# A segment-sum kernel: one source bucket per row of parts 0 and 1 fetched by an indirect row transfer instead of a one-hot product

## The chip, the cores and the metric

The kernel runs on one core of one Trainium2 chip. The metric is the device time of one execution in microseconds. Before the change, three runs took 1863.13, 1871.68 and 1876.03 us, median 1871.68.

## The reference

A graph layer: neighbour features are summed at each destination node, scaled by the inverse degree, and added to the node's own term.

```python
nsum = _segment_sum(x[src], dst, N)
h_neigh = nsum * deg_inv[:, None]
return x @ w_self + h_neigh @ w_neigh
```

There are N = 12500 nodes, 64 features and 800000 edges with random `src` and `dst`. So 800000 rows of x have to be gathered and added up.

## The kernel before, in words

The gather and the sum are both done by TensorE as products with one-hot matrices. For that the edges are sorted first. Each edge becomes a key; keys are grouped into **buckets**: a bucket is a block of 164 destination nodes (there are 77) crossed with a block of 128 source nodes (there are 98), 7546 buckets in all. Each bucket has 128 slots, which hold most of its edges (106 on average); what doesn't fit goes to the "leftovers".

The first 800 us sort: VectorE (DVE) sorts each partition's 6250 keys, then runs are gathered, merged, gathered again and merged, until each of 128 rows holds a fixed number of consecutive buckets. The work is split in three **parts** with 29, 20 and 10 buckets per row (`KPRS`), so part 0 is buckets 0 to 3711, part 1 from 3712 to 6271, part 2 the rest. Only part 0 is ready when the loop over buckets starts. The merges of parts 1 and 2 (L316, L328) are issued on DVE inside that loop, a slice per tile, with a budget per tile that `PACE` gives (an estimate in ns) less what other work of the tile has spent (`self.spent`).

When a part's rows are merged, `find_and_gather` counts bucket limits and fetches a window per bucket (L742), and `decode_buckets` turns the windows into two things: the source numbers within a block (0 to 127), stored to a DRAM table `sl` with one row of 128 per bucket (L794; on SP's queue for part 0, on POOL's for the other parts), and the destination numbers, transposed on TensorE into the SBUF table `dlT`.

The bucket loop is `nodes`. It goes over tiles of 8 buckets (950 tiles):

- `one_hots` (L924) prepares chunks of 28 buckets. Four DMAs on SP's queue (L933) copy the chunk's rows of `sl` to all 128 partitions (`slb`, 3 buffers). DVE compares with the partition's number and gets the source one-hots `ohs` (L935), and compares the columns of `dlT` with a row of numbers for the destination one-hots `ohd` (L940).
- `gather` multiplies each bucket's `ohs` with the 128 node rows of its source block (L966), which yields the bucket's 128 gathered rows in PSUM (`ct`, 8 buckets wide, 3 buffers). ScalarE (ACT) copies them to SBUF as f16 (`xg`, L976); in part 2 DVE takes some of these copies (L974). A row has 128 f16: 64 high parts and 64 low parts of the features.
- `sums` comes a few tiles later and multiplies `xg` with `ohd`, in two halves of 64 partitions, adding up in PSUM `acc` over the 98 buckets of a destination block (L1047). Six blocks (588 buckets, an "octet") share one accumulator; then it is copied out (L1054), multiplied with the weights (L1114), scaled (L1117) and added to the output by an accumulating DMA from POOL's queue (L1123).
- Leftover edges come in groups of 128: `pick` fetches their x rows from the DRAM copy `xt` by an indirect DMA that POOL issues (L997, tile `lx`, 5 buffers), `spread` makes their one-hots (L1006), `add` adds the product (L1015).

The order on each engine is the order in which the Python code issues the instructions. POOL (GpSimd) has one queue for all its work: the leftover gathers, the row gathers of a merge (L565, eight per part, one per tile, each followed by a small memset), the window gathers (L742), the stores to `sl` of parts 1 and 2 (L794) and the outputs (L1123). An instruction that waits holds up all behind it. A leftover gather into a buffer that is still in use waits for the product that reads it (L1015).

## Time and profile before

| | us |
|---|---|
| median of three runs | 1871.68 |
| the profiled execution's own time | 1856.37 |
| its span | 1854.6 |
| bucket loop, parts 0 and 1 | about 805 to 1665 |
| bucket loop, part 2 | about 1665 to 1837 |

| engine | busy us | share of the span |
|---|---|---|
| TensorE products (PE) | 986.6 | 53% |
| VectorE (DVE) | 1718.2 | 93% |
| ScalarE (ACT) | 1116.7 | 60% |
| GpSimd (POOL) | 576.2 | 31% |

How to read the lines below: a line of a group names line, engine, operation, tiles written and read, shapes and count; then the busy time in us and the mean duration in ns; then the idle time of the engine just before these instructions, and what ended it. `ct<-xh,ohs` means that `ct` is written from `xh` and `ohs`. PEld is TensorE's weight load. A table by stretches gives, for each stretch, the busy time and count of each engine, the granted TensorE clock, the share of the DMA engines and GB/s. A wait line reads: who waited, for whom, us in total, times, longest. The chain of waits is followed back from the last instruction; "issue" is time in which the engine waited for nothing that the profile shows.

### The profile page before, as it was taken

The page shows a single profiled execution, that of the slowest core. Times are in us where ns is not written, and L with a number is a line of the kernel's source. Part 1 is how long each engine was busy: PE and PEld are TensorE (multiplying, and loading weights), DVE is VectorE, ACT ScalarE, POOL GpSimd, SP SyncE. Part 2 cuts the span into 40 slices and gives each one's busy share as a digit, 9 for nine tenths or more (in the row PEclk, how much of TensorE's full clock was granted, in tenths as well). Part 3 has the DMA queues.
Part 4 walks back from the last instruction along what each step waited for, and adds up shares of the span by engine and source line. Part 5 has one row for each costly group of instructions (what it writes and reads, how often), then busy time and mean ns, then how long its engine had stood idle before and what let it go on. Part 6 is the DMA issues. An engine that isn't in the chain of part 4 may idle for free.

```text
span 1854.6 us, 54153 instructions
## 1 busy us (share of the span) xinstructions
PE 986.6 (53%) x23413; PEld 851.9 (46%) x23413; DVE 1718.2 (93%) x1718; ACT 1116.7 (60%) x1587; POOL 576.2 (31%) x447
## 2 busy tenths in 40 slices
PE   3046000000000000058979979897898899888996
PEld 1015000000000000057868868776887788777885
DVE  6999999999999999989989999998898799978885
ACT  5263000113001005458979989899999899977885
POOL 2000000055502005404456535473332523532331
PEclk7567555555555555579989999999999999999998
DMA  5207100021002002169978888996889788977894
GB/s 174 54 0 169 39 0 0 38 79 51 18 4 73 10 0 82 47 216 266 274 249 253 251 248 254 296 282 227 264 250 284 234 265 242 326 200 257 274 268 118
DMA packets 176789, 307.79 MB, mean 166 GB/s; under 512 B 127885, under 2 KB 133596, under 8 KB 175772
## 3 DMA queue, kind: packets, MB, share of 16 engines
q1 hardware_dynamic: 98268, 275.58, 44.9%
q0 software_dynamic: 78272, 28.65, 9.6%
q8 instruction: 185, 3.03, 0.7%
q14 instruction: 64, 0.52, 0.1%
HBM read 277.01 MB, written 26.52 MB: 164 GB/s over the span
## 4 chain that ended last, share of the span: by engine, by line
DVE 19%; PE 13%; DMA 11%; issue 10%; SPq 5%; POOL 4%; ACT 4%; DVEq 0%; POOLq 0%; ACTq 0%
DMA slb<-sl 10%; PE ct L966 7%; DVE u L328 7%; PE acc L1047 5%; SPq L933 5%; DVE ohs L935 4%; DVE ohd L940 3%; ACT xg L976 2%; DVE u L362 2%; POOL u L565 1%; POOL lx L997 1%; POOL out L1123 1%; DVE u L316 1%; DMA sl<-l 1%; PE acc L1015 1%
## 5 line engine op out<-in xcount | busy, mean ns | idle before, releaser
L976 ACT ACTIVATE xg<-ct 128x1024 f16<-128x1024 f32 x919 | 862.6, 1074 | 104.4 <-PE ct L966 80.0
L966 PE MATMUL ct<-xh,ohs 128*128 128x128 f16 x7546 | 532.6, 224 | 87.9 <-DVE ohs L935 23.7
L966 PEld LDWEIGHTS <-ohs 128*128 128x128 f16 x7546 | 451.8, 100 | 125.4 <-issue 52.5
L328 DVE TENSOR_TENSOR u<-u 128x1512 f32<-128x1512 f32 (+57 forms) x316 | 425.7, 1362 | 12.9 <-ACT u L312 8.6
L1047 PE MATMUL acc<-ohd,xg 64*128 64x82 f16 x15092 | 395.2, 201 | 47.7 <-ACT xg L976 20.4
L1047 PEld LDWEIGHTS <-xg 64*128 64x128 f16 x15092 | 324.6, 96 | 104.6 <-issue 29.2
L997 POOL DMA_INDIRECT lx<-xt,ls x127 | 232.0, 1826 | 425.6 <-PE acc L1015 352.5
L940 DVE TENSOR_TENSOR ohd<-iota,dlT 128x2296 f16<-128x2296 bf16 x270 | 362.2, 1341 | 0.0
L935 DVE TENSOR_SCALAR ohs<-slb,pidx 128x3584 f16<-128x3584 bf16 x270 | 321.8, 1192 | 40.2 <-DMA slb<-sl 19.0
L509 PE MATMUL stp<-cx,swapa 128*128 128x16 f32 (+1 forms) x12 | 3.1, 335 | 398.0 <-DVE swapa L505 398.0
L260 DVE TENSOR_TENSOR a<-b 128x1040 f32<-128x1040 f32 (+41 forms) x130 | 194.7, 1539 | 3.5 <-DVE b L260 0.5
L260 DVE TENSOR_TENSOR b<-a 128x1040 f32<-128x1040 f32 (+46 forms) x150 | 194.6, 1345 | 3.2 <-ACT a L262 0.4
L538 POOL DMA_INDIRECT u<-d,ixa x48 | 72.5, 1511 | 390.8 <-ACT junka L526 335.4
L509 PEld LDWEIGHTS stp<-cx,swapa 128*128 128x128 f32 x12 | 2.6, 271 | 398.5 <-DVE swapa L505 398.5
L312 ACT ACTIVATE u<-u 128x256 f32<-128x256 f32 (+14 forms) x60 | 33.0, 618 | 170.6 <-DVE u L316 134.8
L1123 POOL DMA_DIRECT2D out<-o x27 | 99.1, 3800 | 103.1 <-ACT o L1117 89.8
L802 PE MATMUL tr<-idb,l 128*128 128x128 bf16 x59 | 7.6, 263 | 188.9 <-ACT l L796 188.9
L262 ACT ACTIVATE b<-a 128x2 f32<-128x2 f32 (+31 forms) x41 | 15.9, 402 | 127.1 <-DVE a L260 120.4
L802 PEld LDWEIGHTS <-l 128*128 128x128 bf16 x59 | 4.3, 114 | 191.2 <-ACT l L796 190.8
L316 DVE TENSOR_TENSOR u<-u 128x2016 f32<-128x2016 f32 (+11 forms) x40 | 61.9, 1563 | 16.2 <-DMA u<-da,ixb 8.8
L262 ACT ACTIVATE a<-b 128x1 f32<-128x1 f32 (+24 forms) x34 | 8.6, 259 | 105.4 <-DVE b L260 99.9
L565 POOL DMA_INDIRECT u<-da,ixb x24 | 36.9, 1539 | 88.6 <-ACT ixb L513 85.0
(158 smaller groups left out, 839.4 us busy)
## 6 DMA issues: line engine op xcount, KB each, us to landing
slb<-sl SPq DMA_DIRECT2D x1076, 224.0 KB
xt<-xh SPq DMA_DIRECT2D x1, 3136.0 KB
out<-o POOLq DMA_DIRECT2D x25, 123.0 KB
own<-os SPq DMA_DIRECT2D x12, 256.0 KB
out<-os SPq DMA_DIRECT2D x12, 256.0 KB
rd<-dst SPq DMA_DIRECT2D x5, 512.0 KB
rs<-src SPq DMA_DIRECT2D x5, 512.0 KB
lx<-xt,ls POOLq DMA_INDIRECT x127
```

The lines of the kernel that those rows point to most:

```text
L260: nc.vector.tensor_tensor(view(dst, lo + sh, [[st, g], [1, l]]), x, y, op=op)
L316: nc.vector.tensor_tensor(at(oth, to, n), x, y, op=op)
L328: nc.vector.tensor_tensor(to, at(cur, ln + lo, n), at(cur, lo + k, n), op=op)
L538: nc.gpsimd.indirect_dma_start(out=u[:, i * w:(i + 1) * w], out_offset=None, in_=src, in_offset=bass.IndirectOffsetOnAxis(ap=self.start[pa ...
L933: nc.sync.dma_start(b[j::4], bass.AP(tensor=src.tensor, offset=src.offset, ap=[[0, 32], [1, n * 128]]))
L935: nc.vector.tensor_scalar(s.rearrange("p c s -> p (c s)"), b, self.pidx[:, :1], None, op0=OP.is_equal)
L940: nc.vector.tensor_tensor(d, self.iota[:, None].to_broadcast(wide), ix, op=OP.is_equal)
L966: nc.tensor.matmul(ct[:, i * 128:(i + 1) * 128], cols[i][0], self.xh[:, (b0 + i) % NB].rearrange("p a f -> p (a f)"), start=True, stop=True)
L976: nc.scalar.activation(xg[:, :cnt * 128], ct[:, :cnt * 128], AF.Copy)
L997: nc.gpsimd.indirect_dma_start(out=x, out_offset=None, in_=self.xt, in_offset=bass.IndirectOffsetOnAxis(ap=self.left[p][1][:, c:c + 1].bit ...
L1047: nc.tensor.matmul(acc[h][:, db % OCT * HN:(db % OCT + 1) * HN], xg[r, i * 128:(i + 1) * 128], d[r], start=db % OCT == 0 and sb == 0, stop ...
L1123: nc.gpsimd.dma_start(out, o[:n, at], accum_op=OP.add)
```

## The change

In parts 0 and 1 one bucket of each row (column 15 of 29, column 11 of 20; `DCOL`) is **direct**: 256 buckets. Their source numbers are not stored to `sl`; the tables' rows move up, so that 7290 source rows are left. In `narrow` the column is transposed on TensorE and turned by three DVE instructions into node numbers (`self.direct`, one column of 128 per bucket row; empty slots get the number N, whose row is zero). In the loop, `bring` issues an indirect DMA on POOL's queue for each direct bucket, at most one per tile and up to 160 buckets ahead (`FETCH`; 12 buffers, `FETCHED`), from `xt` to a tile `xd` of 128 rows of 256 bytes. `sums` uses `xd` in place of the slice of `xg`. So a direct bucket has no source one-hot, no product in `gather` and no part of an eviction; its destination one-hot and its sum stay. A tile now has 8 source buckets and the direct ones between them (914 tiles). The constant `dx` (128 x 384 floats) is loaded on SP's queue.

With it go: source and destination one-hots come from two generators; `pick` counts as taken also the buffers whose product was issued less than `BACK` = 6 tiles ago; the tile `ohl` is two blocks wide instead of six; `PACE` goes from 420 and 405 to 428 and 430.

```diff
@@ -36,12 +36,32 @@
 BASE = [128 * sum(KPRS[:p]) for p in range(NP)]
 TURN = -(-BASE[2] // 28) * 28
 SPARE = TURN - BASE[2]
+DCOL = (15, 11, None)
+KSRC = [k - (c is not None) for k, c in zip(KPRS, DCOL)]
+SBASE = [128 * sum(KSRC[:p]) for p in range(NP)]
+DIRECT = {BASE[p] + r * KPRS[p] + c: (p, r) for p, c in enumerate(DCOL) if c is not None for r in range(128)}
+NSRC = NBID - len(DIRECT)
+assert max(DIRECT) < BASE[2]
+FETCH = 160
+FETCHED = 12
 assert 128 * KPRS[2] < BASE[1]
 NCOL = 128 * sum(KPRS)
 NCNT = [(k + 3) // 4 for k in KPRS]
...
+OCT = 6
+TILES = []
+for o in range(0, NBID, OCT * NB):
+    b = o
+    while b < min(o + OCT * NB, NBID):
+        e, n = b, 0
+        while e < min(o + OCT * NB, NBID) and (e in DIRECT or n < 8):
+            n += e not in DIRECT
+            e += 1
+        TILES.append((b, e - b))
+        b = e
+START = [next(t for t, (b, n) in enumerate(TILES) if b + n > BASE[p]) for p in range(NP)]
 SUP = 8
 COUNTED = 4600
 WAIT = 20e3
@@ -49,7 +69,7 @@
 NSUP = 128 // SUP
 LENA = [l[3:] for l in LENS]
 LENB = [l[4:] for l in LENS]
-PACE = (0, 420, 405)
+PACE = (0, 428, 430)
 LROW = [l[-1] for l in LENS]
 LEAD = 616
 EXT = 36
@@ -71,8 +91,9 @@
...
+DCH = 28
 HELD = 5
-OCT = 6
+BACK = 6
...
@@ -168,6 +189,8 @@
                -(t - np.uint32(1)).view(np.float32)]
     out = {"c1": c1, "cx": np.concatenate(cx, 1).astype(np.float32)}
     assert out["cx"].shape == (128, NCX)
+    at = np.array([BASE[p] + np.arange(128) * KPRS[p] + (c or 0) for p, c in enumerate(DCOL)])
+    out["dx"] = np.tile((at % NB * 128 - N).reshape(1, -1), (128, 1)).astype(np.float32)
     for p in range(NP):
         kpr = KPRS[p]
         b = BASE[p] + np.arange(128)[:, None] * kpr + np.arange(kpr)[None]
@@ -409,6 +432,8 @@
...
+        self.dx = keep.tile([128, NP, 128], F32, name="dx")
+        self.direct = {}
         self.junkb = keep.tile([128, JUNKB], BF, name="junkb")
         self.idb = keep.tile([128, 128], BF, name="idb")
         make_identity(nc, self.idb)
@@ -479,6 +504,7 @@
...
+                nc.sync.dma_start(self.dx.rearrange("p a r -> p (a r)"), self.I["dx"])
                 for p in range(NP):
                     nc.sync.dma_start(self.c2[p], self.I[f"c2_{p}"])
         self.runs, self.portions = sort_runs(nc, (a, b), RUN)
@@ -790,8 +816,22 @@
             l16 = vp.tile([128, 4, 128], BF, name="l16", bufs=2 if part else 4)
             nc.scalar.activation(l16[:, :n], w, AF.Sign, bias=self.edge[:, :1], accum_out=self.cnt[:, c:c + 1])
             nc.scalar.activation(l16[:, :n], w, AF.Copy)
-            rows = self.sl[BASE[part]:BASE[part] + 128 * kpr].rearrange("(r k) s -> r k s", k=kpr)
-            (nc.gpsimd if part else nc.sync).dma_start(rows[:, k:k + n], l16[:, :n])
+            m, to = n, k
+            if DCOL[part] is not None:
+                m -= DCOL[part] == k + n - 1
+                to -= DCOL[part] < k
+                assert not k <= DCOL[part] < k + m
+            rows = self.sl[SBASE[part]:SBASE[part] + 128 * KSRC[part]].rearrange("(r k) s -> r k s", k=KSRC[part])
+            (nc.gpsimd if part else nc.sync).dma_start(rows[:, to:to + m], l16[:, :m])
+            if m < n:
+                ps = mps.tile([128, 128], BF, name="dt", tag="ct", bufs=3)
+                nc.tensor.transpose(ps, l16[:, m], self.idb)
+                u = vp.tile([128, 128], F32, name="du")
+                nc.vector.tensor_tensor(u, ps, self.dx[:, part], op=OP.add)
+                nc.vector.scalar_tensor_tensor(u, ps, 128.0, u, op0=OP.is_lt, op1=OP.mult)
+                self.direct[part] = self.keep.tile([128, 128], U32, name=f"dix{part}")
+                nc.vector.tensor_scalar(self.direct[part], u, float(N), None, op0=OP.add)
+                self.spent += 800
             l16 = vp.tile([128, 4, 128], BF, name="l16", bufs=2 if part else 4)
             nc.scalar.activation(l16[:, :n], vk, AF.Copy)
             return l16
@@ -921,60 +961,95 @@
         self.left[part] = (place, s)
         yield 1
 
-    def one_hots(self, pool):
-
-
-        nc = self.nc
-        for c in range(0, NBID, 28):
-            n = min(28, NBID - c)
+    def source_hots(self, pool):
+
+
+        nc = self.nc
+        for c in range(0, NSRC, 28):
+            n = min(28, NSRC - c)
             b = pool.tile([128, 28 * 128], BF, name="slb", bufs=3)[:, :n * 128]
             src = self.sl[c:c + n]
             for j in range(4):
                 nc.sync.dma_start(b[j::4], bass.AP(tensor=src.tensor, offset=src.offset, ap=[[0, 32], [1, n * 128]]))
-            s = pool.tile([128, 28, 128], FH, name="ohs", bufs=3)[:, :n]
-            nc.vector.tensor_scalar(s.rearrange("p c s -> p (c s)"), b, self.pidx[:, :1], None, op0=OP.is_equal)
-            d = pool.tile([128, 14, HN, 2], FH, name="ohd", bufs=4)[:, :n // 2]
+            s = pool.tile([128, 28 * 128], FH, name="ohs", bufs=3)[:, :n * 128]
+            nc.vector.tensor_scalar(s, b, self.pidx[:, :1], None, op0=OP.is_equal)
+            yield [s[:, j * 128:(j + 1) * 128] for j in range(n)]
+
+    def dest_hots(self, pool):
+
+
+        nc = self.nc
+        for c in range(0, NBID, DCH):
+            n = min(DCH, NBID - c)
+            d = pool.tile([128, DCH // 2, HN, 2], FH, name="ohd", bufs=4)[:, :n // 2]
             at = c % TURN
             wide = [128, n // 2, HN, 2]
             ix = self.dlT[:, at:at + n].rearrange("p (c t) -> p c t", t=2)[:, :, None, :].to_broadcast(wide)
             nc.vector.tensor_tensor(d, self.iota[:, None].to_broadcast(wide), ix, op=OP.is_equal)
-            yield [(s[:, j], d[:, j // 2, :, j % 2]) for j in range(n)]
+            yield [d[:, j // 2, :, j % 2] for j in range(n)]
 
     def nodes(self, pool, aps, mps):
 
 
         nc = self.nc
-        source = self.one_hots(pool)
-        ready = []
+        sources, dests = self.source_hots(pool), self.dest_hots(pool)
+        ready, spare = [], []
         pend = []
         late = []
         done = []
+        added = []
         acc = None
 
         turn = 0
+
+        left = [NSRC, NBID]
+        fetch = iter(sorted(DIRECT.items()))
+        coming = [next(fetch)]
+        held = {}
+
+        def bring(b0, most):
+
+            while most and coming and coming[0][0] <= b0 + FETCH and coming[0][1][0] in self.direct:
+                b, (p, r) = coming.pop()
+                coming.extend(islice(fetch, 1))
+                held[b] = pool.tile([128, 128], FH, name="xd", bufs=FETCHED)
+                nc.gpsimd.indirect_dma_start(
+                    out=held[b], out_offset=None, in_=self.xt,
+                    in_offset=bass.IndirectOffsetOnAxis(ap=self.direct[p][:, r:r + 1], axis=0))
+                most -= 1
 
         def gather(b0, cnt, vector):
 
             nonlocal turn
             ct = aps.tile([128, 1024], F32, name="ct", bufs=3)
             ahead = AHEAD - 8 * vector
-            while len(ready) < min(cnt + ahead, NBID - b0):
-                ready.extend(next(source))
-            cols = ready[:cnt]
-            del ready[:cnt]
-            for i in reversed(range(cnt)):
-                nc.tensor.matmul(ct[:, i * 128:(i + 1) * 128], cols[i][0],
-                                 self.xh[:, (b0 + i) % NB].rearrange("p a f -> p (a f)"), start=True, stop=True)
+            own = [b for b in range(b0, b0 + cnt) if b not in DIRECT]
+            num = len(own)
+            while len(ready) < min(num + ahead, left[0]) or len(spare) < min(cnt + ahead, left[1]):
+                if len(ready) <= len(spare) and len(ready) < left[0]:
+                    ready.extend(next(sources))
+                else:
+                    spare.extend(next(dests))
+            cols = ready[:num]
+            dest = spare[:cnt]
+            del ready[:num]
+            del spare[:cnt]
+            left[0] -= num
+            left[1] -= cnt
+            for i in reversed(range(num)):
+                nc.tensor.matmul(ct[:, i * 128:(i + 1) * 128], cols[i],
+                                 self.xh[:, own[i] % NB].rearrange("p a f -> p (a f)"), start=True, stop=True)
             xg = pool.tile([128, 1024], FH, name="xg", bufs=6)
-            if vector and (len(ready) < min(8 + ahead, NBID - b0 - cnt) or NBID - b0 < 56):
+            if vector and (len(ready) < min(8 + ahead, left[0]) or NBID - b0 < 56):
                 turn += 1
             else:
                 vector = False
             if vector and turn % 2:
-                nc.vector.tensor_copy(xg[:, :cnt * 128], ct[:, :cnt * 128])
+                nc.vector.tensor_copy(xg[:, :num * 128], ct[:, :num * 128])
             else:
-                nc.scalar.activation(xg[:, :cnt * 128], ct[:, :cnt * 128], AF.Copy)
-            return b0, xg, [d for _, d in cols]
+                nc.scalar.activation(xg[:, :num * 128], ct[:, :num * 128], AF.Copy)
+            parts = {b: xg[:, i * 128:(i + 1) * 128] for i, b in enumerate(own)}
+            return b0, [parts[b] if b in parts else held.pop(b) for b in range(b0, b0 + cnt)], dest
 
         uses = []
...
         def pick(b0):
-            if self.picked == len(done) or len([u for u in uses if u[5]]) >= HELD:
+            busy = len([u for u in uses if u[5]]) + len([n for n in added if n > len(done) - BACK])
+            if self.picked == len(done) or busy >= HELD:
                 return
             u = next((u for u in uses if not u[5]), None)
             if u and u[1] in self.left and b0 + LEAD >= u[4] * NB:
@@ -1001,18 +1077,20 @@
 
         def spread(u):
             o, p, c, f, e = u[:5]
-            u[7] = pool.tile([128, 2, OCT * HN], FH, name="ohl", bufs=HELD)
+            assert e - f <= 2
+            u[7] = pool.tile([128, 2, 2 * HN], FH, name="ohl", bufs=HELD)
             n = slice((f - o * OCT) * HN, (e - o * OCT) * HN)
-            nc.vector.tensor_scalar(u[7][:, :, n], self.wide.rearrange("p (h n) -> p h n", h=2)[:, :, n],
+            nc.vector.tensor_scalar(u[7][:, :, :(e - f) * HN], self.wide.rearrange("p (h n) -> p h n", h=2)[:, :, n],
                                     self.left[p][0][:, c:c + 1], -float(o * (OCT * HN + 4096)),
                                     op0=OP.subtract, op1=OP.is_equal)
             self.spent += 300
 
         def add(u, stop=False):
             o, _, _, f, e = u[:5]
+            added.append(len(done))
             n = slice((f - o * OCT) * HN, (e - o * OCT) * HN)
             for h in range(2):
-                nc.tensor.matmul(acc[h][:, n], u[5], u[7][:, h, n], start=False, stop=stop)
+                nc.tensor.matmul(acc[h][:, n], u[5], u[7][:, h, :(e - f) * HN], start=False, stop=stop)
 
         def extras(b0, cnt):
             o = b0 // (OCT * NB)
@@ -1040,11 +1118,11 @@
...
-            for i, d in enumerate(cols):
+            for i, (x, d) in enumerate(zip(xg, cols)):
                 db, sb = divmod(b0 + i, NB)
                 for h in range(2):
                     r = slice(h * H, (h + 1) * H)
-                    nc.tensor.matmul(acc[h][:, db % OCT * HN:(db % OCT + 1) * HN], xg[r, i * 128:(i + 1) * 128], d[r],
+                    nc.tensor.matmul(acc[h][:, db % OCT * HN:(db % OCT + 1) * HN], x[r], d[r],
                                      start=db % OCT == 0 and sb == 0, stop=False)
...
-        tiles = []
-        for o in range(0, NBID, OCT * NB):
-            end = min(o + OCT * NB, NBID)
-            tiles += [(b0, min(8, end - b0)) for b0 in range(o, end, 8)]
+        tiles = TILES
+        bring(0, 8)
         for t, (b0, cnt) in enumerate(tiles):
+            bring(b0, 1)
             pend.append(gather(b0, cnt, self.changed))
             if (len(pend) > 5) if self.changed else t % 2:
                 while len(pend) > (3 if self.changed else 2):
-                    b0 = pend[0][0]
+                    b0, cnt = pend[0][0], len(pend[0][2])
                     if sums(pend.pop(0)):
                         break
-                extras(b0, 8)
+                extras(b0, cnt)
             else:
                 pick(b0)
             b0 = tiles[t][0]
@@ -1353,7 +1430,7 @@
                 if last != "gather" or not n % 2 and self.picked < n - 1:
                     last = next(chain, None)
                     if last is None:
-                        assert n < BASE[part] // 8 - 12
+                        assert n < START[part] - 12
                         chain = None
                         self.changed = part == NP - 1
                         work.close()
```

## The prediction

> **What bounds the kernel now.** I read the table by stretches first, because the change touches only the bucket loop. The cuts are where the loop reaches part 1 (about 1310 us) and part 2 (about 1665 us).
>
> ```profile
> 805.00:1310.00 505.00, 439.53 (x11040) 387.50 (x11038) 480.68 (x582) 461.72 (x590) 231.94 (x129) 0.96 0.86 261
> 1310.00:1665.00 355.00, 315.07 (x7912) 279.29 (x7909) 322.76 (x402) 326.29 (x429) 138.60 (x85) 0.96 0.85 259
> 1665.00:1855.00 190.00, 156.63 (x4194) 141.25 (x4191) 152.11 (x163) 142.11 (x170) 52.60 (x28) 0.96 0.76 229
> ```
>
> The columns are PE, PEld, DVE, ACT, POOL, granted clock, DMA share, GB/s. In the 860 us of parts 0 and 1 DVE is busy 803.4 us (93%), ACT 788.0 (92%), PE 754.6 (88%), the DMA engines 86%; POOL has room (43%). So the stretch runs on DVE, with ACT next to it, and DVE is idle for only 56.6 us. That idle time is the most that relief elsewhere can give back. Next I read the groups that the change shortens or copies:
>
> ```profile
> L976 ACT ACTIVATE xg<-ct 128x1024 f16<-128x1024 f32 x919 | 862.6, 1074 | 104.4 <-PE ct L966 80.0
> L966 PE MATMUL ct<-xh,ohs 128*128 128x128 f16 x7546 | 532.6, 224 | 87.9 <-DVE ohs L935 23.7
> L997 POOL DMA_INDIRECT lx<-xt,ls x127 | 232.0, 1826 | 425.6 <-PE acc L1015 352.5
> L935 DVE TENSOR_SCALAR ohs<-slb,pidx 128x3584 f16<-128x3584 bf16 x270 | 321.8, 1192 | 40.2 <-DMA slb<-sl 19.0
> L1123 POOL DMA_DIRECT2D out<-o x27 | 99.1, 3800 | 103.1 <-ACT o L1117 89.8
> ```
>
> The leftover gather (L997) is the same transfer as the new ones: 128 rows of 256 bytes out of xt. It costs POOL 1.83 us each, and POOL stood 352.5 us ahead of it, waiting for a buffer that PE was still reading. Then the waits inside the two stretches, for what DVE lacks:
>
> ```profile
> DVE ohs L935 <- DMA slb<-sl: 6.3, 7, 1.9
> DVE ohs L935 <- PE ct L966: 3.5, 5, 1.3
> DVE u L316 <- DMA u<-da,ixb: 7.3, 1, 7.3
> ...
> DVE ohs L935 <- PE ct L966: 12.0, 10, 2.9
> DVE u L316 <- DMA lx<-xt,ls: 7.0, 1, 7.0
> DVE xg L974 <- PE ct L966: 4.5, 2, 3.2
> DVE ohs L935 <- DMA slb<-sl: 4.7, 5, 2.3
> ```
>
> DVE waits 11.0 us for the broadcast of source numbers, 20.0 us for PE, and 14.3 us at L316 for the row gathers of a merge. The chain of waits shows what made the second of those late:
>
> ```profile
> 1420.96 12.97 issue
> ...
> 1434.16 1.49 POOL lx L997
> ...
> 1438.64 1.65 POOL u L565
> ...
> 1457.54 1.00 DVE u L316
> ```
>
> POOL stands 13 us in front of a leftover gather; the eight row gathers (L565) are queued behind it, and the merge on DVE waits.
>
> **The change part by part.** *Source one-hots.* 7546 buckets become 7290, so 270 chunks of 28 become 261: 9 × 1.192 = **−10.7 us** of DVE, in the stretch where DVE leads. The destination one-hots stay at 270. *Index columns.* Two groups of three small DVE instructions and two transposes. The nearest row is
>
> ```profile
> L917 DVE TENSOR_SCALAR lz<-lk 128x64 f32<-128x64 f32 (+2 forms) x3 | 0.8, 254 | 0.0
> ```
>
> so six at 0.254 give 1.5 us, and I take **+1.5**. The added load of the constant on SP stands on SP behind the load of cx, ahead of the sort, and the sort covers it; uncovered it would be one transfer of the size of that of cx.
>
> *Products and evictions.* A tile now holds 8 source buckets plus the direct ones between them: counted from the lists of tiles in the code, 950 become 914. That is 36 × 1.074 = 38.7 us less for ACT and 256 × 532.6/7546 = 18.1 us less for PE. Neither leads; each pays only where DVE waits for PE (20.0 us). The bounds are 0 and −20; PE loses 2.4% of its time and ACT 4.9%, not all that makes these waits, so I take **−6**.
>
> *The waits of the leftover gathers.* The count of buffers taken now includes those added within the last 6 tiles, so POOL no longer stands in front of L997 and L565 is not held up by it. That can take away the 14.3 us at L316. But among the eight row gathers, one a tile, there are now two to four direct ones, 4 to 8 us. Bounds −14.3 and +8; I take **−7**.
>
> *POOL's share of DVE's time.* A DVE instruction can be held up by a gather:
>
> ```profile
> L935 DVE TENSOR_SCALAR ohs<-slb,pidx x270: 679/1146/2475, 803.4 to 1832.0; 128x3584 f16<-128x3584 bf16 x135
> L997 POOL DMA_INDIRECT lx<-xt,ls x127: 938/1561/5031, 836.5 to 1798.0; - x127
> L742 POOL DMA_INDIRECT v<-d,ix x30 | 45.1, 1505 | 35.0 <-ACT ix L762 24.4 <-ACT xg L976 7.6 <-issue 3.0
> L565 POOL DMA_INDIRECT u<-da,ixb x16 | 25.8, 1614 | 12.6 <-ACT ixb L513 10.2 <-issue 2.4
> ```
>
> L935 has a median of 1146 and a mean of 1192 ns, with a tail to 2475: 46 ns × 270 = 12.4 us of excess. If the 127 + 30 + 16 gathers and the 27 output transfers caused it, each costs DVE 62 ns, and 256 more cost 15.9 us. The lower bound is 0, if the tail has another cause. I take **+13**, near the upper one.
>
> *The broadcast and the new rows on the DMA engines.*
>
> ```profile
> q1 hardware_dynamic: 98268, 275.58, 44.9%
> q0 software_dynamic: 78272, 28.65, 9.6%
> slb<-sl SPq DMA_DIRECT2D x1076, 224.0 KB
> ```
>
> Removed are 36 transfers of 224 KB, 8.1 MB at 1854.6 × 0.449/275.58 = 3.02 us per MB: −24 us of all engines. Added are 32768 rows of 256 bytes, 8.39 MB: by q0's time per packet (1854.6 × 0.096 × 16/78272 = 36.4 ns) 74.5 us, by its time per MB (6.2 us) 52 us. The net is +28 to +50 us over 860, so the share goes from 0.86 to 0.89 to 0.92. It is hidden as long as three broadcast buffers run ahead of L935; the 11.0 us of waits grow. Bounds 0 and +14; I take **+5**.
>
> *The gathers themselves, 256 × one POOL instruction.* They are issued 160 buckets ahead. The first stretch of the products' own counts gives the lead:
>
> ```profile
> 1310.00:1665.00 355.00, 184.48 (x2596) 156.28 (x2597) 0.96 0.85 259
> ```
>
> 160 × 355/2596 = 21.9 us. The transfer itself is hidden by that lead. What is queued behind it on POOL are L997, L565, L742, the stores to sl and the outputs; who waits for a late one is PE, in the sums, and behind that all products, so ACT. Whether POOL keeps up depends on the time from start to start:
>
> ```profile
> L997 POOL DMA_INDIRECT lx<-xt,ls x36 | 61.7, 1713 | 141.4 <-PE acc L1015 137.6 <-issue 2.3 <-PE ct L966 1.2
> ...
> 1667.30 1.07 POOL L997 DMA_INDIRECT lx<-xt,ls  x1 [20.62 <-PE acc L1047]
> 1668.68 0.99 POOL L997 DMA_INDIRECT lx<-xt,ls  x1 [0.30 <-issue]
> ...
> 1673.93 1.66 POOL L997 DMA_INDIRECT lx<-xt,ls  x1 [0.30 <-DMA lx<-xt,ls]
> ```
>
> Five in a row start 6.63/4 = 1.66 us apart. In part 0 POOL then has 231.9 + 129 gaps × 0.30 + 128 × 1.66 = 483 us to do in 505: it fits. In part 1 it is 138.6 + 85 × 0.30 + 128 × 1.66 = 377 in 355 us plus the lead of 21.9, that is, exactly at the edge. With the mean of part 1 (1.713 + 0.30 = 2.01) it is 422, 45 us too much. The bounds are 0 and +45; the burst is the nearest row, since a gather that is queued behind others behaves like it, so I take **+3** for bursts that meet.
>
> The pace of the merges (428 and 430 per tile for 420 and 405) goes over fewer tiles; the merges themselves are the same work, so nothing. **Sum**: −10.7 + 1.5 − 6 − 7 + 13 + 5 + 3 = **−1.2 us**. The profiled execution took 1856.37 us (span 1854.6 and 1.8 around it) and would take 1855.2. The median of the runs, 1871.68, stands 15.3 us above it; on that footing the forecast is 1870.5, **no change**. One per cent, 18.7 us, is about what a measurement of this kernel can tell from none.
>
> The Trainium skill, page "SBUF — State Buffer", section "Who interferes with whom", says that DVE in certain fast modes and GpSimd exclude each other from a shared port for a whole instruction. Its section on the two sides of SBUF has such a transfer at 620 ns alone and about 3100 ns beside a DVE copy. With 3.1 us a gather, part 1 would have about 560 us to do on POOL, an estimate from that page, and the change would lose over 180 us. The trace agrees that gathers spread (938 to 5031 ns) and that L935 has a tail, but its median gather is 1561 ns.
>
> **The rivals.** *POOL becomes the bound in part 1 (slower).* Place: the sums of part 1, whose PE instructions wait for a direct gather. It decides from a start-to-start time of (355 + 21.9 − 138.6 − 25.5)/128 = 1.66 us. Price: at 2.01 us +45 us, 1915; at 1.85 us, halfway, +24, 1894. Behind it would be gathers and L935 that hold each other up: L935 alone takes 321.8 us of the loop, and a gather that meets it has to stand aside, up to the 5031 ns of the longest. For it: the mean of 1713 ns and the edge just worked out. Against it: the bursts, and POOL's 352.5 us of waiting, which go. The Trainium skill describes such a lock on its page "SBUF — State Buffer", section "Who interferes with whom".
>
> *ACT and PE were the true limit (faster).* The merges may be filler on DVE that moves up into gaps. Then DVE's idle time of waits goes (−20.0 and −14.3), DVE's own work falls by 9.2, and the tail of L935 stays as it is: −43 at the very most, with the DMA waits against it. With two thirds of it, −28: 1844. For it: ACT at 92% loses 38.7 us. Against it: DVE above 93%, and DMA and POOL both fuller.
>
> *The DMA engines fill up (slower, small).* At a share of 0.92 on average, some stretches are full, and L935 waits for its broadcasts. If its 11.0 us become two and a half times as much, that is 16.5 more than now and 11.5 more than my +5: 1882.
>
> **How the numbers follow.** No change 0.42, which has the small DMA case in it; faster by the relief of ACT and PE 0.30; slower 0.28, of which POOL 0.22 and DMA with the L935 tail 0.06. Chances: faster 0.30, same 0.42, slower 0.28. All the lower bounds of the terms together would be −43.5 us (1828), all the upper ones without POOL's +28.7 (1900), with it +73.7 (1945); the terms do not all fall to one side, and the forecast's own range is 1853 to 1890. To leave out no more than 2 in 10, the range reaches to 1840 (just past the faster case) and to 1908 (between the two prices of POOL's).
>
> **What would show it.** Right: 261 instructions of L935's kind with a mean at or above 1200 ns; 914 evictions; DVE busy in parts 0 and 1 within 10 us of 803; POOL near or above 90% in part 1; PE's waits for direct gathers under 10 us; L316 waiting less than 14 us. Wrong: PE waiting tens of microseconds for a direct tile (POOL's case), or DVE's idle time in both parts down to 25 us or less (the faster case), or a mean gather above 2 us with no wait behind it.

## The result, and the profile after

The changed kernel took 2054.74 to 2070.27 us in four runs, median 2058.98; the kernel before, beside it, 1863.13 to 1882.86, median 1873.86. The ratio is **1.102, 95% interval 1.098 to 1.106**. The forecast was 1870.5, no change. The profiled execution took 2054.74 us (span 2052.8), 198.4 more than the one of before.

The table by stretches of the changed kernel, at the same cuts as before (PE, PEld, DVE, ACT, POOL, granted clock, DMA share, GB/s):

```profile
805.00:1310.00 505.00, 417.06 (x9469) 355.92 (x9470) 414.03 (x463) 384.39 (x478) 365.19 (x211) 0.88 0.76 228
1310.00:1665.00 355.00, 277.76 (x6097) 231.56 (x6096) 251.18 (x324) 256.72 (x334) 258.35 (x173) 0.85 0.68 204
```

In the same 860 us DVE does 665.2 us of work where it did 803.4, and PE issues 15566 products where it issued 18952. Part 1 now begins at about 1416 us, part 2 at 1867. Nothing is as busy as DVE was, POOL has taken 253 us more, and the DMA engines have more room than before. So the loop isn't held by an engine's work but by waits. The groups:

```profile
L1050 ACT ACTIVATE xg<-ct 128x1024 f16<-128x1024 f32 x885 | 842.3, 1053 | 316.7 <-PE ct L1040 144.6
L1040 PE MATMUL ct<-xh,ohs 128*128 128x128 f16 x7290 | 560.6, 231 | 87.1 <-issue 45.7
...
L1016 POOL DMA_INDIRECT xd<-xt,dix x256 | 425.8, 1663 | 129.0 <-issue 63.4
...
L975 DVE TENSOR_SCALAR ohs<-slb,pidx 128x3584 f16<-128x3584 bf16 (+1 forms) x261 | 312.7, 1198 | 144.0 <-PE ct L1040 49.6
```

ACT and DVE stand idle behind PE. And PE, by the waits of the loop:

```profile
PEld L1125 <- issue: 168.1, 274, 11.7
...
PE acc L1125 <- issue: 115.4, 194, 11.5
PEld L1040 <- issue: 111.6, 184, 23.0
...
PEld L1125 <- DMA xd<-xt,dix: 6.6, 3, 5.2
```

"issue" means that nothing in the profile ended the pause. PE waits 6.6 us for direct tiles and many times that for nothing that can be seen. In the timeline of PE it looks like this:

```profile
1429.96 0.27 PE L1125 MATMUL acc<-ohd,xg 64*128 64x82 f16 x4 [0.49 <-issue]
1430.68 0.23 PE L1125 MATMUL acc<-ohd,xd 64*128 64x82 f16 x2 [0.46 <-issue]
1430.73 0.25 PE L1125 MATMUL acc<-ohd,xg 64*128 64x82 f16 x3
1431.47 0.26 PE L1125 MATMUL acc<-ohd,xg 64*128 64x82 f16 x4 [0.50 <-issue]
```

About four products, then half a microsecond of nothing, every 0.7 us. I call these **bare stalls**: pauses of PE above 0.3 us, from 800 us on, ahead of a product that has no semaphore to wait for. Counted in the trace there are 225 of them, 125.2 us; the trace of before has 25, 21.9 us.

The changed kernel doesn't show them everywhere. The experiments came in groups; a group ran on one chip, with the kernel before beside it. In them the changed kernel took 1958.84 us once (14 bare stalls) and 2038.68 once (211), while the kernel before stayed within 1856 and 1883. So about 95 us of the result go with the bare stalls, and about 95 us are there without them. The experiments take the two apart. Where no interval is given, a time is that of one execution, good to about 1%, so the difference of two such times is good to some 20 us.

### The profile page after: what moved, and what is told of

It is laid out like the page before. It is cut to its first block, busy times and chain, and to the rows that moved or that the text cites. A ratio compares the mean times of both kernels' runs of the same rounds, so it can differ in the third digit from the quotient of the medians.

```text
span 2052.8 us, 53879 instructions
## 1 busy us (share of the span) xinstructions
PE 1075.2 (52%) x23159; PEld 898.2 (44%) x23159; DVE 1712.7 (83%) x1713; ACT 1098.4 (54%) x1553; POOL 957.8 (47%) x703
## 3 DMA queue, kind: packets, MB, share of 16 engines
q0 software_dynamic: 86464, 37.03, 10.3%
## 4 chain that ended last, share of the span: by engine, by line
PE 31%; issue 12%; ACT 6%; DMA 4%; POOL 3%; DVE 3%; SPq 1%; another core or an unknown queue 1%; DVEq 0%; ACTq 0%; POOLq 0%
PE ct L1040 16%; PE acc L1125 13%; ACT xg L1050 4%; DMA slb<-sl 2%; DMA xd<-xt,dix 2%; POOL xd L1016 1%; PE po L1191 1%; SPq L973 1%; PE acc L1093 1%; POOL out L1200 1%; DVE ohd L988 1%; POOL lx L1073 1%; DVE ohs L975 1%; DMA sl<-l 1%
## 5 line engine op out<-in xcount | busy, mean ns | idle before, releaser
L1050 ACT ACTIVATE xg<-ct 128x1024 f16<-128x1024 f32 x885 | 842.3, 1053 | 316.7 <-PE ct L1040 144.6
L1040 PE MATMUL ct<-xh,ohs 128*128 128x128 f16 x7290 | 560.6, 231 | 87.1 <-issue 45.7
L1040 PEld LDWEIGHTS <-ohs 128*128 128x128 f16 x7290 | 465.2, 104 | 135.9 <-issue 111.6
L1125 PE MATMUL acc<-ohd,xg 64*128 64x82 f16 x14580 | 445.2, 207 | 129.2 <-issue 98.5
L1016 POOL DMA_INDIRECT xd<-xt,dix x256 | 425.8, 1663 | 129.0 <-issue 63.4
L1125 PEld LDWEIGHTS <-xg 64*128 64x128 f16 x14580 | 350.7, 99 | 212.7 <-issue 149.9
L975 DVE TENSOR_SCALAR ohs<-slb,pidx 128x3584 f16<-128x3584 bf16 (+1 forms) x261 | 312.7, 1198 | 144.0 <-PE ct L1040 49.6
L1073 POOL DMA_INDIRECT lx<-xt,ls x127 | 204.2, 1608 | 170.4 <-PE acc L1093 103.8
L339 DVE TENSOR_TENSOR u<-u 128x2016 f32<-128x2016 f32 (+11 forms) x40 | 62.1, 1564 | 12.5 <-DMA u<-da,ixb 12.1
L591 POOL DMA_INDIRECT u<-da,ixb x24 | 30.8, 1282 | 87.8 <-ACT ixb L539 83.4
```

Of the source, the lines that this page charges most:

```text
L339: nc.vector.tensor_tensor(at(oth, to, n), x, y, op=op)
L975: nc.vector.tensor_scalar(s, b, self.pidx[:, :1], None, op0=OP.is_equal)
L1016: nc.gpsimd.indirect_dma_start(out=held[b], out_offset=None, in_=self.xt, in_offset=bass.IndirectOffsetOnAxis(ap=self.direct[p][:, r:r + 1 ...
L1040: nc.tensor.matmul(ct[:, i * 128:(i + 1) * 128], cols[i], self.xh[:, own[i] % NB].rearrange("p a f -> p (a f)"), start=True, stop=True)
L1050: nc.scalar.activation(xg[:, :num * 128], ct[:, :num * 128], AF.Copy)
L1073: nc.gpsimd.indirect_dma_start(out=x, out_offset=None, in_=self.xt, in_offset=bass.IndirectOffsetOnAxis(ap=self.left[p][1][:, c:c + 1].bit ...
```

## The experiments

**First group: what the direct tiles cost, and what they save.** `held` is the dictionary of fetched tiles.

```diff
 plain load on SP:   -nc.gpsimd.indirect_dma_start(out=held[b], ...)
                     +nc.sync.dma_start(held[b], self.xt[b % NB * 128:b % NB * 128 + 128])
 gathers unread:     +still = pool.tile([128, 128], FH, name="still", bufs=1)
                     the sums of the direct buckets read it, and it holds zeros
 no gathers:          as gathers unread, and no indirect_dma_start in bring
 before + gathers:    the kernel before, with 256 gathers into 6 buffers that nobody reads
```

> The direct tiles come by a plain load of a block of xt on SP's queue in place of the indirect transfer on POOL (other rows of x, so the sums differ). Everything else is as after the change: PE's waits for the tile, the 914 tiles, the pace, the rule for the leftovers. If the gathers on POOL starve PE (my theory now), the time falls to 1850 to 1885 us and PE's gaps without a wait fall from 125 us to about 25. If POOL merely brings the tiles too late, the same, but then the kernel after should show PE waiting for xd, and it shows 12 us. If PE's additional waits or the new tiles and order cost the time, it stays at 2040 to 2070.

> All 256 gathers are issued as after the change, but no product reads them: the sums read one constant zero tile for the direct buckets (their edges are left out). If the gathers themselves starve PE, 2040 to 2070 us. If late tiles or PE's waits for them cost the time, 1850 to 1890.

> As the unread kernel, and the gathers are not issued either: what the removed one-hots, products and evictions are worth with nothing paid for them (the edges of the direct buckets are left out). If the gathers cost all of it, 1835 to 1865 us; POOL's load falls back to that of before. If the new tiles, the pace or the rule for the leftovers cost the time, above 1950.

> The kernel before, unchanged in its products, with 256 gathers of 128 rows added at the places where the change has them, into 6 buffers that nobody reads. If the gathers themselves starve PE, 2020 to 2090 us with over 100 us of PE's gaps without a wait. If it is anything else of the change, 1870 to 1895 (the tail of the one-hot instructions and POOL's queue).

Measured, with 1856.1 for the kernel before: plain load on SP 1886.91, gathers unread 1966.46, no gathers 1848.63, before with gathers 1946.07 (between the two ranges given for it). All that the change takes away came to 7.5 us, which one run of each can't tell from nothing. 256 gathers that nobody reads cost 118 us on the changed kernel and 90 on the one before. The four had 13 to 23 bare stalls, no more than the kernel before (25), so many gathers alone don't bring the stalls. The plain load's 38 us over no gathers are a price of its own, on the queue that carries the broadcasts. DVE's waits in that run, with 17.1 us at the same place without gathers:

```profile
DVE ohs L975 <- DMA slb<-sl: 50.4, 31, 7.8
```

**Second group: do the bare stalls come from reading the gathered tile?**

```diff
 copy:        +parts[b] = pool.tile([128, 128], FH, name="xc", bufs=6)
              +nc.scalar.activation(parts[b], held.pop(b), AF.Copy)
 plain POOL:  -nc.gpsimd.indirect_dma_start(out=held[b], ...)
              +nc.gpsimd.dma_start(held[b], self.xt[b % NB * 128:b % NB * 128 + 128])
 both:        the plain load on SP is read, the gather goes to 8 buffers that nobody reads
 part 0:      -DCOL = (15, 11, None)
              +DCOL = (15, None, None)
```

> The changed kernel with one more step: ACT copies each direct tile from its gather buffer into a tile of its own (256 copies of 128 x 128), and PE's sums read the copy. PE then waits for no gather and POOL's buffers are freed by ACT. The gathers, their number and their order stay. Changed kernel: 2055 us, 225 stalls of PE over 0.3 us without a wait, 125 us in them. Theory A (PE is held because it reads or waits for what POOL's gather has brought, or because POOL waits for PE): the stalls go to about 20 and the time falls to that of the unread gathers, 1966, or with 256 copies of some 0.25 us on ACT up to 1985. Theory B (the rate of gathers alone starves PE, and that the unread run had none was because it ran slower): stalls stay over 100 and the time stays at 2040 to 2080.

> The changed kernel with each direct tile loaded by a plain DMA on POOL's queue (the 128 consecutive rows of its source block, not the rows by index, so the sums are of other rows); same order, same buffers, read by PE. Theory A in its narrow form (the indirect operation is what PE's reading collides with): no stalls, and POOL's instruction is shorter than the 1.66 us of a gather, so POOL's queue is not late: about the plain load on SP's queue, 1887, or less since SP's broadcasts are free of them, 1850 to 1890. If anything that POOL's own queue brings holds PE up: stalls of PE over 100 and over 1950 us. POOL's share of parts 0 and 1 (0.73 in the changed kernel) tells how far its queue was the reason.

> The changed kernel with both: each direct tile is loaded by a plain DMA on SP's queue and read by PE (other rows than the indexed ones), and the indirect gather is issued as before, into 8 buffers that nobody reads. So PE has direct tiles and waits for them, POOL has all its gathers, but PE doesn't read what the gathers bring. Theory A: no stalls without a wait (about 20); the time is that of the unread gathers, 1966, plus up to the 38 us of the plain load over no gathers: 1965 to 2005. Theory B: stalls over 100, 2050 or more.

> The changed kernel with direct buckets in part 0 alone (column 15 of 29; 128 gathers in place of 256). If POOL's rate is what counts, part 0 (a gather per 3.9 us of the loop) costs less than half of the changed kernel's 198 us over the profile of before, as part 1 (one per 2.8 us) is the denser: 1900 to 1940. If every gather has its price, 0.75 us each: half, 1955. If part 0 were harmless: 1850 to 1865.

Measured, with 1863.77 for the kernel before: copy 2073.55 with 227 bare stalls (137 us), both 2073.83 with 268 (144 us), part 0 alone 1971.58 with 155 (94 us; above all three ranges given for it), plain POOL **1861.72** with 46. Theory A fell: with the copy PE waits for no gather, and stalls as much (PE's waits in the run with the copy):

```profile
PEld L1129 <- issue: 166.9, 285, 2.2
```

But in "both" the gathers were unread, as in the first group, where PE didn't stall. Either the kernels differ or the groups do. And plain loads on POOL, with the same bytes in the same order, cost nothing that two runs can tell.

**Third group: the same kernels side by side.**

```diff
 after again, unread again: no edit
 plain slow:  the plain load on POOL, and behind it
              +nc.gpsimd.memset(pool.tile([128, 500], F32, name="busy", bufs=1), 0.0)
 before, plain leftovers (the kernel before):
              -nc.gpsimd.indirect_dma_start(out=x, ...)
              +nc.gpsimd.dma_start(x, self.xt[u[3] % NB * 128:u[3] % NB * 128 + 128])
```

> The changed kernel as it is, beside the next run on the same chip. With the copy, with the plain load next to unread gathers, and in part 0 alone PE had its stalls without a wait (155 to 268 of them), in two earlier runs with unread gathers it had none (18, 19), and those two ran on another chip. If the kernels differ: this one 2055 with 225 stalls, the unread one 1966 with 19. If the chips differ: both have the stalls, or neither has.

> The changed kernel with its gathers issued and not read (the sums of the direct buckets read a tile of zeros), once more, on the chip that runs the changed kernel. If the kernels differ: 1966 and about 20 stalls of PE without a wait. If what differed was the chip: within 20 us of the changed kernel on the same chip, with like many stalls.

> The plain load on POOL's queue (1862, 0.94 us of POOL each, other rows than the indexed ones), and behind each a memset of 128 x 500 floats on POOL, some 0.6 us, that nobody reads, so that POOL is as long at a direct bucket as with a gather (1.57). Theory P (POOL's time: its queue runs late, as I had first put it): the time goes to that of the gathers, 1966 to 2055. Theory I (the indirect operation itself takes something from PE, some 0.8 us each: 108 us for 128 in part 0 alone, 198 for 256): the time stays at 1855 to 1885.

> The kernel before, with its 127 leftover gathers as plain loads of 128 consecutive rows on POOL's queue (so the sums of the leftovers are of other rows). Theory I, 0.8 us for each indirect operation: 100 us faster, 1765. Theory P: POOL was busy 31% in the kernel before and held up little: 1845 to 1865. If only a dense run of gathers hurts: no change either.

Measured, with 1863.23 before: changed kernel **1958.84** with 14 bare stalls, unread 1957.80 with 15, plain slow 1880.47, before with plain leftovers 1844.34. The last is 19 us faster, not the 100 of a price of 0.8 us for each indirect operation. Plain slow lies in the range of theory I, but it took POOL 1.42 us a bucket from start to next start, not as long as a gather, as its expectation had it; it decides nothing. So the bare stalls come with the group and not with the reading, and reading the tile costs nothing that two runs can tell. What is left, 95.6 us, comes from the gathers themselves; whether as work on POOL or as indirect operations, the next groups ask. The waits of the changed kernel in this group:

```profile
PEld L1125 <- DMA xd<-xt,dix: 86.4, 29, 8.1
PE acc L1125 <- DMA xd<-xt,dix: 82.2, 28, 8.0
...
DVE u L339 <- DMA u<-da,ixb: 27.7, 2, 15.6
```

(PE and its weight load wait at the same time; the two are not added.) If nobody reads the direct tiles, the lateness lands on what is queued behind them, the leftover gathers and a merge's rows (waits of the unread run):

```profile
PEld L1097 <- DMA lx<-xt,ls: 57.8, 17, 12.1
...
DVE u L339 <- DMA u<-da,ixb: 31.7, 2, 19.5
```

The times are the same, 1958.84 and 1957.80: whoever it is that waits, the loss is the same.

**Fourth and fifth groups: how full is POOL's queue?**

```diff
 plain twice:  two plain loads on POOL (the second unread), and a memset of 128 x 100
 after, plain leftovers: the 127 leftover gathers as plain loads on POOL, the 256 direct gathers stay
 part 0 again: no edit
 plain full:   as plain twice, with a memset of 128 x 350 and 4 buffers for the unread load
 after, third time: no edit
 before, BACK: the kernel before; pick counts buffers added in the last 6 tiles, 8 buffers lx
```

> In place of each gather POOL issues two plain loads (the second into 8 buffers that nobody reads) and a memset of 128 x 100 floats: 0.93 + 0.93 + 0.20 us, as long as a gather takes with the gap ahead of it (1.80 + 0.31), and no indirect operation. The direct sums are of other rows than the indexed ones. Theory P (POOL's queue is full: 371 us of work and 46 of gaps in the 860 us of parts 0 and 1 before, plus 256 x 2.06 = 944, 84 more than there is): 1935 to 1965. Theory I (the indirect operation itself): 1860 to 1890.

> The changed kernel, its 256 direct gathers as they are, and the 127 leftover gathers as plain loads on POOL's queue (0.75 us in place of 2.07; the sums of the leftovers are of other rows). Theory P: 86 of them lie in parts 0 and 1, 114 us of POOL's time, so its sum falls from 955 to 841 us, under the 860: 1845 to 1875. Theory I: 127 of 383 indirect operations fewer, a third of the loss at most: 1920 or more. On a chip where PE stalls without a wait, up to 95 us more by either, and the stalls (over 100) show it.

> Direct buckets in part 0 alone, once more; it took 1971.58 with 155 stalls of PE without a wait. POOL's sum for part 0's 505 us: 232 of work, about 29 of gaps, 128 x 2.1 = 269: 530, 25 us too much, which part 1 gives back. If the stalls belong to the chip: fewer than 40 here and 1855 to 1890. If they belong to this kernel: over 100 and 1950 to 1990.

> As the run with two plain loads, with a memset of 128 x 350 floats in place of 128 x 100 and 4 buffers for the unread load: by the memsets so far (0.45 us for 100, 0.74 for 500) some 0.25 us longer, so about 2.0 us of POOL for a direct bucket, start to next start, and no indirect operation (other rows than the indexed ones). Theory P (a full queue, whatever fills it): where POOL's waits in parts 0 and 1 go under 60 us, 1925 to 1965. Theory I (half of the 95 us belongs to the indirect operation): 1890 to 1915 though POOL hardly waits.

> The changed kernel on this chip: 1955 to 1965 with fewer than 40 stalls of PE without a wait, or 2050 to 2075 with over 150.

> The kernel before with 8 buffers for the leftover gathers instead of 5, and a buffer counted as free only 6 tiles after its product was issued (the rule BACK of the change). POOL then waits less at a leftover gather (264 us in the loop before), and what is queued behind it, the merges' row gathers and the windows, comes earlier. If that wait is what the plain leftover loads took off: 1840 to 1850, ratio 0.987 to 0.994. If it was the length of the operation: 1855 to 1865, ratio 0.997 to 1.003.

Measured, fourth group (before 1860.37): plain twice 1893.64, changed kernel with plain leftovers 1884.16, part 0 again **1911.56 with 13 bare stalls**, where the same kernel had 1971.58 with 155. Fifth group (before, 13 runs, median 1866.93): plain full 1925.54 with 46 bare stalls, changed kernel 2038.68 with 211, before with BACK 1878.03 (ratio 1.0064, 1.0037 to 1.0090: slower than both ranges given for it, so that wait on POOL was not worth removing). Plain twice and the changed kernel with plain leftovers each fell between the ranges of their two theories, and part 0 again had the few stalls of the one answer but took 22 us more than it allowed.

From each trace I joined POOL's records from the first sum of part 0 to the last of part 1 and counted pauses up to 0.45 us as filled, since the 0.30 us ahead of a gather has no releaser:

| kernel | POOL filled, us of us | share | us over the kernel before of its group |
|---|---|---|---|
| no gathers | 424 of 855 | 50% | -7.5 |
| plain POOL | 548 of 864 | 63% | -2 |
| plain slow | 670 of 888 | 75% | +17 |
| plain twice | 750 of 904 | 83% | +33 |
| plain full | 802 of 925 | 87% | +59 |
| changed, plain leftovers | 814 of 894 | 91% | +24 |
| before + gathers | 886 of 962 | 92% | +90 |
| changed, unread | 905 of 965 | 94% | +95 |
| changed | 920 of 967 | 95% | +96 |

The share alone doesn't set the loss: 91% cost 24 us and 92% cost 90, since a full queue lengthens the stretch that it is a share of. The work itself tells more. Up to 814 us of it, less than the 855 to 875 that parts 0 and 1 take without the added work, the loss was 59 us or less; from 886 us on it was 90 or more.

With all 256 direct gathers left in, two thirds of the indirect operations, and only the leftovers shorter, three quarters of the loss are gone (+24 for +96): it is not a price of each indirect operation. And part 0 alone fills POOL where the gathers are, and not in part 1: its part 0 lasted 569 us, where the profile of before has 518, its part 1 359 for 357 (part 0 again, stretches, columns as above):

```profile
805.00:1310.00 505.00, 406.21 (x10050) 362.65 (x10050) 437.82 (x497) 404.83 (x511) 424.15 (x224) 0.90 0.81 241
1310.00:1665.00 355.00, 305.97 (x7616) 270.10 (x7610) 313.70 (x402) 320.43 (x421) 172.40 (x103) 0.94 0.83 253
```

Against the theory that a full queue costs the same whatever fills it: plain twice was to fill the queue and missed it, because POOL's plain loads overlap. The three groups

```profile
L1016 POOL DMA_DIRECT2D xd<-xt x256 | 210.3, 877 | 58.3 <-DVE top L900 36.0 <-DMA out<-o 9.9 <-PE acc L1125 9.4
L1017 POOL DMA_DIRECT2D xu<-xt x256 | 209.1, 871 | 28.6 <-DMA out<-o 24.1 <-DMA da<-u 2.2 <-issue 1.6
L1018 POOL MEMSET busy<- 128x100 f32 x256 | 115.4, 451 | 0.0
```

add up to 2.20 us, but from start to next start, where they follow each other, a direct bucket took 1.77; the gathers of the changed kernel take 2.09. The loss grows with the work on POOL, but not smoothly: plain full lost more (+59) than the changed kernel with plain leftovers (+24), with 802 us of work for 814 and POOL unfilled for 123 us; it is in a group with bare stalls. The memsets also lengthened the source one-hots, to 1240 ns in plain slow and 1214 in plain full: 13 and 6 us on DVE that are not POOL's queue. A queue filled to 95% without a direct gather was not reached, so that plain work would cost as much as the gathers is not shown.

## Why the prediction was wrong

**The step that failed** is the one on the gathers themselves: "the burst is the nearest row, since a gather that is queued behind others behaves like it, so I take +3". It took 1.66 us from start to start, from five leftover gathers in a row, and gave 2.01 only to the rival. Measured in the third group, where work follows a direct gather at once: 2.09 (1.80 for the operation, 0.30 ahead of the next). With that, the prediction's own sum for part 0 is 231.9 + 38.7 + 128 × 2.09 = 538 us of POOL in 505, 33 too much, and for part 1 138.6 + 25.5 + 267.5 = 432 in 376.9, 55 too much. Together **88 us; measured 95.6**. So the rival "POOL becomes the bound" was the case, with its price mis-sized: its place was not part 1 alone, because at 2.09 part 0 doesn't fit either. Of PE's 82.2 us of waits for direct tiles, 48 lay in part 0, which lasted 565 us for 518; part 1 lasted 402 for 357. That the sum comes so near is in part luck: it has 970 us of work for POOL, the records 920, and POOL stood for the other 47 us of the stretch.

A row that prices part 0 lay in the profile of before, the leftover gathers of that stretch (805 to 1310 us):

```profile
L997 POOL DMA_INDIRECT lx<-xt,ls x70 | 138.7, 1981 | 178.0 <-PE acc L1015 130.3 <-DVE ls L905 37.1 <-issue 7.5
```

With 1.98 + 0.30 = 2.28 us for a gather part 0 has 58 us too much, and with the 2.01 of part 1 the prediction's own 45 come to it: some 102 us.

Why was the burst the wrong row? What a gather takes depends on what DVE does beside it, and the burst lay at 1667 to 1675 us, in part 2, where DVE at first had a row of instructions of some 0.2 us each, as these of the kernel before:

```profile
1667.05 0.17 DVE L911 TENSOR_SCALAR lt<-lt 128x19 int32<-128x19 int32 x1
1667.26 0.25 DVE L912 TENSOR_SCALAR lt<-lt 128x19 int32<-128x19 int32 x1
1667.54 0.18 DVE L913 CUSTOM_DVE_ANT_0 lq<-lq,lt 128x38 uint16<-128x38 uint16 x1
```

POOL, and then DVE, of the changed kernel in the third group (start, duration, instruction, idle time ahead):

```profile
1109.19 0.94 POOL L1016 DMA_INDIRECT xd<-xt,dix  x1 [0.30 <-issue]
1110.44 0.94 POOL L1016 DMA_INDIRECT xd<-xt,dix  x1 [0.30 <-issue]
...
1118.38 2.26 POOL L1016 DMA_INDIRECT xd<-xt,dix  x1 [0.30 <-issue]
1120.95 3.62 POOL L1016 DMA_INDIRECT xd<-xt,dix  x1 [0.30 <-issue]
1124.87 3.41 POOL L1016 DMA_INDIRECT xd<-xt,dix  x1 [0.30 <-issue]
```

```profile
1114.30 2.51 DVE L975 TENSOR_SCALAR ohs<-slb,pidx 128x3584 f16<-128x3584 bf16 x1 [6.23 <-PE ct L1040]
...
1118.11 1.34 DVE L988 TENSOR_TENSOR ohd<-iota,dlT 128x2296 f16<-128x2296 bf16 x1
1119.38 1.14 DVE L975 TENSOR_SCALAR ohs<-slb,pidx 128x3584 f16<-128x3584 bf16 x1
...
1122.04 1.34 DVE L988 TENSOR_TENSOR ohd<-iota,dlT 128x2296 f16<-128x2296 bf16 x1
1123.30 1.14 DVE L975 TENSOR_SCALAR ohs<-slb,pidx 128x3584 f16<-128x3584 bf16 x1
1124.36 1.34 DVE L988 TENSOR_TENSOR ohd<-iota,dlT 128x2296 f16<-128x2296 bf16 x1
```

While DVE stands idle for 6.23 us, gathers take 0.94 us; while DVE runs one instruction behind the other, 2.3 to 3.6. Over that trace, 118 of the 383 gathers (direct and leftover) took under 1.05 us, mean 0.95, and lay beside an instruction of DVE for 0.35 us on average; 148 took up to 2 us, mean 1.54, and had DVE beside them for 1.43; 117 took over 2 us, mean 2.96, and had DVE beside them for 2.90. Which instruction it is counts too: 103 of the 117 end 0.12 to 0.18 us after a source one-hot (L975) has ended, and none so soon after a destination one-hot or a step of a merge. The Trainium skill, page "SBUF — State Buffer", section "Who interferes with whom", puts it as a rule: where a DMA seems stalled by a DVE instruction, it was one that GpSimd issues, and GpSimd lacked the port to write its descriptors. The trace agrees that gathers stretch beside DVE, with the times above; the port itself no run here shows. The page's 3.1 us would be too much here as a mean, as the prediction said; it is near the 2.96 of the long third. So in a stretch where DVE was 93% busy, the price of a gather is that beside a busy DVE.

**The other 95 us** are in no step and no rival. What the runs show of the bare stalls:

| indirect gathers in the loop | bare stalls, groups 2 and 5 and the result's profile | groups 1, 3 and 4 |
|---|---|---|
| 173 (none or plain loads for the direct ones; before with BACK) | 46, 46, 71 | 13 to 36 |
| 301, 302 (part 0; plain leftovers) | 155 | 13, 16 |
| 429 | 211 to 268 | 14 to 19 |

More than a hundred of them take many gathers, and a group that has them; the profile of the kernel before, with 25, belongs to none of the five. They don't need the gathered tile to be read (both, 268), nor PE to wait for it (copy, 227). Groups 2 and 4 ran on chips of the same number, so that doesn't tell them apart. In the 18 us from 1429 on, where the timeline of PE above lies, the DMA table of the changed kernel's profile has packets of two queues alone:

```profile
q1 hardware_dynamic: 643, 3.04, 52.5%
q0 software_dynamic: 843, 0.52, 15.4%
```

and in the next 18 us three of the instruction queue as well:

```profile
q8 instruction: 3, 0.05, 1.0%
```

In the 15 places of that profile where six or more bare stalls follow each other within 2.5 us, 119 us in all, the two queues that bring instructions started 9 packets, where the loop's mean would give 21. That fits a PE that waits for instructions, and as well a PE that stands for another reason and so uses fewer. It is argued and not shown; what differs between the groups stays open.

**The other steps.** *Source one-hots*: 261 with a mean of 1198 ns, 312.7 us in place of 321.8: −9.1 for −10.7. DVE's work in parts 0 and 1 came out as forecast (803 ± 10; the third group's run from 811 to 1778 us, its parts 0 and 1):

```profile
811.00:1778.00 967.00, 766.03 (x18983) 680.33 (x18980) 804.54 (x981) 771.17 (x994) 800.79 (x464) 0.91 0.78 234
```

It is the same work in 967 us, where the kernel before took 874 (808 to 1683), with POOL at 83% before its pauses. *Evictions*: 885 on ACT and 29 on DVE, 914. *The tail of L935, +13*: it did not grow; the mean is 1182 to 1198 ns in every run with 256 direct gathers, 1192 before. It is the gather that takes longer, not DVE. *The savings together* were −22 (−10.7, +1.5, −6, −7); the kernel without gathers gained 7.5, one run beside one run. *The leftover waits, −7*: the wait at the merge (L339) was 27.7 us in the third group, not under 14, because the row gathers stand behind direct ones. *DMA engines, +5*: q0 has 86464 packets for 78272, so 8192 came for 32768 rows of 256 bytes, half of them 2048 bytes long; I had priced 32768. As many bytes as plain loads on POOL cost nothing that can be told (1861.72 beside 1863.77). *PE's waits for direct tiles under 10 us*, the sign that was to show it right, held in the profile of after (6.6) although the kernel was 10% slower: with the bare stalls PE was so late that POOL, busy for 73% of the 860 us, kept ahead of it.

No version with direct buckets beats the kernel before by more than a run can tell: even with nothing fetched the gain was 7.5 us.

## What to carry to other kernels

Price an instruction of a shared in-order queue by its mean in the stretch where it will stand, with the pause ahead of it, and not by a burst found where its neighbours rest; then add up the whole queue per stretch, not only the new work. Here what DVE does beside a gather sets its price: 0.94 us beside an idle DVE, 1.5 to 3 us beside a busy one. And a queue at the edge of what fits is no small term: the three kernels with POOL filled to between 83 and 91% lost 24 to 59 us.

## What the runs showed that was not expected

- The changed kernel took 1958.84 us in one group and 2038.68 to 2070.27 elsewhere, the kernel before 1856 to 1883 everywhere: the bare stalls of PE, half a microsecond after some four products, grow with the number of gathers in some groups and don't come in others.
- PE's granted clock in the changed kernel's profile was 0.88 and 0.85 in the two stretches, where it was 0.96, and a product (L1040) took 231 ns in place of 224.
- A plain load of 128 rows on POOL's queue took 0.75 to 0.94 us of POOL on average, an indirect one in the loop 1.54 to 2.03, and only ahead of the indirect one stands the pause of 0.30 us. Two rows of the lists of groups, the plain loads of the second group and the gathers of the third:

```profile
L1016 POOL DMA_DIRECT2D xd<-xt x256 | 194.5, 935 | 82.1 <-PE acc L1123 36.3 <-DVE top L900 35.9 <-DMA xd<-xt 8.5
```

```profile
L1016 POOL DMA_INDIRECT xd<-xt,dix x256 | 461.8, 1804 | 114.5 <-issue 57.4 <-DVE top L900 36.2 <-PE ct L1040 7.5
```
